# Channel slots of a fused attention and spectral-mix kernel: second pair's scores behind the first's

## The chip, the cores and the metric

The kernel runs on one core of a Trainium2 chip. The metric is the time on the device in microseconds (us); lower is better. Three runs of a kernel give its median, and one more execution was profiled.

## What is computed

Inputs q, k, v are (8, 12, 448, 64): batch 8, 12 heads, 448 positions, head width 64. Everything is float32.

```python
scores = cap * tanh(q @ k.T / sqrt(64) / cap)        # cap = 30
attn = exp(scores - max(scores)); attn /= sum(attn) + 1e-9
x = (attn @ v)                                       # heads side by side: (8, 448, 768)
theta = x @ w_theta
y = w_tok_r @ (x * cos(theta)) + w_tok_i @ (x * sin(theta))
u = x + y
out = u + max(u @ w_ch, 0)
```

## The kernel before, in words

The work is a list of slots. Slot s computes the scores of "step" s, which is four heads: two pairs i = 0, 1 of two heads h each. Beside them stands a share of the other work of one batch b. From slot 4 on three slots belong to each batch: part 0 computes theta, part 1 the token mix (mx), part 2 the channel product (ch). Three steps fill the 768 columns of a later batch. The words of a script (the lists PARTS and OTHER) give the order in which instructions are queued; each engine works through its own in that order. PARTS[2] is the script of slots 9, 12, 15, 18 and 21, which are called channel slots here; slots 6 and 24 have scripts of their own.

Words of the script that matter here:

- S0 to S3: score products of the four "bursts" of a slot. S0 holds chunks (0, 0) and (0, 1), that is pair 0 and its first and second 128 positions of k. S1 holds (0, 2) and None, the last 64 positions of both pairs. S2 holds (1, 0) and (1, 1), S3 holds (1, 2). A chunk is three products per head: k high x q high, k low x q high, k high x q low; None is one product in full float32.
- t0 to t3 and e0 to e3: ScalarE's tanh out of the banks and exp in place, of a burst each.
- V0, W, Vr: attn @ v of the step before (accumulators named a); cV0, cV1: ScalarE's copies of them to tiles X.
- a0a to a1b and F0, F1: VectorE adds up exp over the chunks, transposes and sums (folds). Rb: a small product of folds with diagonal gives the sums r; I inverts them and spreads them by DMA (bc); N and N- multiply X by bc.
- Pa1, Pb1: the high and low halves of q and of k of the slot's second pair; Pa0, Pb0: of the next slot's first pair. For an odd k both halves are VectorE's.
- u0 to u5: high half (ScalarE) and low half (VectorE) of the channel product's input; X0 to X5 the same for the next batch's theta.
- C0 to C5: channel product, 18 matmuls of 128x448 each; c0 to c5: its end on VectorE, and the DMA out.

Banks: psS is one tile of four banks (tag s) for S0, S1 and S2; psM has four single banks that a, r, mx, th, ch and S3's two tiles use in turn. The halves of k have one room each (tags kh, kl), so the second pair's k can be halved only when the first pair's last product has read them. Other halves, raw q and k, X, and bc come from 22 small rooms, handed out in the order in which they come free. The cap is 30, so the branch without the maximum runs (general is False).

Of the kernel before, what the change touches and what calls it, by code (L numbers as in the profile page):

```python
# [38 lines left out]
FLIP = (1,)  # L39

FOLD = (0, 1, 2)

FILL = {"branch": 10, "S0": 2, "t0": 8, "t1": 4}

# [34 lines left out]
def softcap_attn_then_spectral_mix(ctx, tc, qk2, v, cap, w_theta, w_tok, w_ch, outT):  # L79
# [16 lines left out]
    theta_words = w_theta.bitcast(I32).rearrange("m p j (n two) -> m p j n two", two=2)  # L96
    w_theta, w_ch = (w.rearrange("m p j n -> m p (j n)") for w in (w_theta, w_ch))

    singles = const.tile([P, 8], F32, name="singles")
    cap_sb, qscale, quarter, curve, wide_cap = (singles[:, n : n + 1] for n in range(5))  # L100
    wide_cap = wide_cap[:1, :].bitcast(I32)
    ones_sb = singles[:, 5:]
    nc.sync.dma_start(cap_sb, cap.broadcast_to([P, 1]))

    nc.vector.tensor_scalar(cap_sb.bitcast(I32), cap_sb.bitcast(I32), 0x7FFFFFFF, None, op0=ALU.bitwise_and)
# [24 lines left out]
    def load_consts():  # L130
        nc.gpsimd.memset(ones_sb[:, :1], 1.0)
        nc.gpsimd.memset(ones_sb[:, 1:], 0.0)
        for i in range(2):
            nc.gpsimd.memset(ones_sb[i * D : (i + 1) * D, i + 1 : i + 2], 1.0)
        nc.gpsimd.memset(diagonal, 0.0)
        for m in range(4):
            nc.gpsimd.affine_select(out=diagonal, in_=diagonal, pattern=[[0, 2], [-1, 32]], compare_op=ALU.not_equal, fill=1.0, base=-32 * m, channel_multiplier=1)
# [125 lines left out]


    BURSTS = (((0, 0), (0, 1)), ((0, 2), None), ((1, 0), (1, 1)), ((1, 2),))

    def load_raw(k, part, last=False):
        t = raw[k, part] = small.take([P, S], F32, f"{'qk'[part]}{k}", last=last)
# [16 lines left out]
    def prep_q(k):  # L285

        if 2 * WHOLE <= k < 2 * NS:
            Q[k, "q"] = halves(raw[k, 0], [P, S], small.take, f"q{k}", by_scalar(k))

    def prep_k(k):  # L290

        if 2 * WHOLE <= k < 2 * NS:
            t = raw.pop((k, 1))
            Q[k, "k"] = halves(t[:, :REST], [P, REST], lambda shape, dtype, name: wk.tile(shape, dtype, tag=f"k{name[-1]}", name=name, bufs=1), f"k{k}", by_scalar(k))
            if k % 2 == 0:
                Q[k, "r"] = wk.tile([P, S - REST], F32, tag="kr", name=f"r{k}", bufs=1)
                nc.vector.tensor_copy(Q[k, "r"], t[:, REST:])
            small.give(t)
            if k + 1 < 2 * NS:
                load_raw(k + 1, 1, k % 2 == 0 and by_scalar(k) and k > 2 * LEAD + 6)  # L300

    def scores(s, n):
        if n == 3 and s not in (1, LEAD + 1):
            t = spt[s, n] = [psM.tile([P, 512], F32, tag="m", name=f"s{s}_{n}{h}") for h in range(2)]
        else:
            t = spt[s, n] = psS.tile([P, 2, 2, 512], F32, tag="s", name=f"s{s}_{n}")
        for u, what in sorted(enumerate(BURSTS[n]), key=lambda at: at[1] is not None):
            for i in (0, 1) if what is None else what[:1]:
                k = 2 * s + i
                rows, cols = (slice(i * D, (i + 1) * D), slice(REST, S)) if what is None else (slice(0, P), slice(what[1] * P, (what[1] + 1) * P))  # L310
                out = [t[h][rows] if isinstance(t, list) else t[rows, u, h] for h in range(2)]
                if what is None and (k, "r") in Q:
                    products = ((Q.pop((k, "r")), raw[k, 0]),)
                elif what is None or s < WHOLE:
                    products = ((raw[k, 1][:, cols], raw[k, 0]),)
                else:
                    kk, qq = Q[k, "k"], Q[k, "q"]
                    products = [(kk[a][:, cols], qq[c]) for a, c in ((0, 0), (1, 0), (0, 1))]
                for m, (kk, qq) in enumerate(products):
                    for h in range(2):  # L320
                        rows = slice(h * D, (h + 1) * D)
                        nc.tensor.matmul(out[h][:, :S], kk[rows], qq[rows], start=m == 0, stop=m == len(products) - 1)  # L322
        k = 2 * s + n // 2
        if n in ((1, 3) if s else (1, 2)) and s < WHOLE:
            for part in range(2):
                small.give(raw.pop((k, part)))
        elif s >= WHOLE and n % 2:
            for t in Q.pop((k, "q")):
                small.give(t)
            if n == 1:  # L330
                for i in range(2):
                    small.give(raw.pop((k + i, 0)))
                if k + 2 < 2 * NS:
                    load_raw(k + 2, 0)
                    load_raw(k + 3, 0)

    def direct(s):
        return state["general"] or s < DIRECT

    def tanh(s, n):  # L340
        m = len(BURSTS[n])
        if m == 2:
            pp = large.take([P, 2, 2, S], F32, f"p{s}_{n}", EXPS if s < LEAD - 1 else None, s >= LEAD and n != 2)
            users[s, n] = [pp, {0: {"V0"}, 1: {"Vr", "V0"}, 2: {"W"}}[n] | (({"Ra", "Rb"}, {"Ra"}, {"Ra", "Rb"})[n] if direct(s) else set())]
        else:
            pp = wk.tile([P, 1, 2, S], F32, tag="p1", name=f"p{s}_{n}", bufs=1)
        for u, what in enumerate(BURSTS[n]):
            U[s, what] = pp[:, u]
        t = spt.pop((s, n))
        for h, each in enumerate(t if isinstance(t, list) else ()):  # L350
            nc.scalar.activation(pp[:, 0, h], each[:, :S], AF.Tanh, scale=qscale)
        if not isinstance(t, list):
            nc.scalar.activation(pp, t[:, :m, :, :S], AF.Tanh, scale=qscale)  # L353
        U[s, "t", n] = pp

    def used(s, word):
# [75 lines left out]
    def sums(s, word):  # L432
        if folded(s):
            if word == "Rb":
                r = state["r"] = psM.tile([P, 512], F32, tag="m", name=f"r{s}")
                for i in range(2):
                    nc.tensor.matmul(r[i * D : (i + 1) * D, : 2 * S // 32], diagonal.rearrange("p a j -> p (a j)"), folds[:, i], start=True, stop=True)
            return
        if not direct(s):
            if word == "Ra":  # L440
                return
            rounds, last = [([pst.pop((s, i)) for i in range(2)], False)], True
        else:
            rounds = [([U[s, (i, c)] for i in range(2)], False) for c in ((0, 2) if word == "Ra" else (1,))]
            if word == "Ra":
                rounds.append(([U[s, None]] * 2, True))
            last = word == "Rb"
        first = word == "Ra" or not direct(s)
        if first:
            state["r"] = psM.tile([P, 512], F32, tag="m", name=f"r{s}")  # L450
        r = state["r"]
        for n, (tiles, rest) in enumerate(rounds):
            for i in range(2):
                for h in range(2):
                    m = 32 * (2 * i + h)
                    nc.tensor.matmul(r[m : m + 32, :S], ones_sb[:, (i + 1 if rest else 0)][:, None].broadcast_to([P, 32]), tiles[i][:, h, :],  # L456
                                     start=first and n == 0, stop=last and n == len(rounds) - 1)

    def invert(s):
        r = state.pop("r")  # L460
        ri = small.take([P, S], F32, f"ri{s}") if direct(s) and not state["general"] else wk.tile([P, S], F32, tag="ps", name=f"ri{s}", bufs=2)
        if not folded(s):
            nc.vector.transpose(out=ri, in_=r[:, :S])
        few = wk.tile([P, S // 32], F32, tag="few", name=f"few{s}", bufs=1)
        each = ri.rearrange("p (c j) -> p c j", j=32)[:, :, 0]
        if state["general"]:
            nc.vector.tensor_scalar_add(few, each, 1e-9)
            nc.vector.reciprocal(few, few)
        elif folded(s):
            for m in range(4):  # L470
                rows, n = slice(32 * m, 32 * m + 32), S // 32
                nc.vector.reciprocal(few[rows], r[rows, n * (m % 2) : n * (m % 2) + n])  # L472
        else:
            nc.vector.reciprocal(few, each)
        nc.vector.transpose(out=ri, in_=few.unsqueeze(2).broadcast_to([P, S // 32, 32]))
# [12 lines left out]

    XHL = {}

    def split_x(b, j, name):
        if j % 2 == 0:
            XHL[name, b, j // 2] = large.take([P, 2, 2, S], F32R, f"{name}{b}_{j}")
        t = XHL[name, b, j // 2][:, j % 2]
        nc.scalar.copy(t[:, 0, :], X[b, j])
        nc.vector.tensor_tensor(t[:, 1, :], X[b, j], t[:, 0, :].bitcast(F32), op=ALU.subtract)  # L496

    def proj(b, wh, wl, m, name, of):
        acc = psM.tile([P, 512], F32, tag="m", name=f"{name}{b}_{m}")
# [117 lines left out]
    def chan_out(b, m):  # L617
# [15 lines left out]
    )  # L633
    OTHER = {
        0: "v S0 t0 q0 q1 w0 e0 S1 t1 S3 e1 w1 S2 t2 Vr^ e2 V0^ t3 S0> w2 e3 w3",
# [16 lines left out]
    def pipeline(general):  # L652
        state["general"] = general
        nc.scalar.activation(curve, quarter, AF.Tanh)
        def run(s, b, word):
# [63 lines left out]
                    fold(s, i)  # L719
            elif name == "w":  # L720
                weights(WEIGHTS.get((s, i), ""))
            elif name == "u":
                split_x(b, i, "us")
            elif name == "X":
                if b + 1 < B:
                    split_x(b + 1, i, "xs")
# [78 lines left out]
```

## Time and profile before

| | |
|---|---|
| median of 3 runs | 867.83 us (867.19 to 867.86) |
| profiled execution, own time | 867.0 us |
| its span, first to last instruction | 865.2 us |
| TensorE busy | 857.3 us, 99% of the span |
| VectorE busy | 716.5 us, 83% |
| ScalarE busy | 593.3 us, 69% |
| GpSimd busy | 112.5 us, 13% |
| granted TensorE clock | 0.999 of full speed |

Engines in the rows: PE is TensorE's matmuls, PEld its weight loads, DVE is VectorE, ACT ScalarE, POOL GpSimd, SP SyncE. A row of a timeline says start, length, engine, line of the code, operation, output <- inputs, shapes, how many instructions were merged, and in brackets how long the engine stood idle before it and what ended that. Ends of matmuls are modelled, so a matmul's start is the firmer number. The chain that ended last is followed back from the last instruction.

### The profile page before, as it was taken

How to read it: one execution, taken by the hardware profiler on the slowest of the kernel's cores; microseconds unless marked ns; L12 is line 12 of the kernel's file. 1: busy time of each engine (PE TensorE's matmuls, PEld its weight loads, DVE VectorE, ACT ScalarE, POOL GpSimd, SP SyncE). 2: the span in 40 equal slices, each digit the busy share in tenths (PEclk: the TensorE clock that was granted, in tenths of full speed). 3: DMA queues.
4: the chain of work that ended last, by engine and by line, in shares of the span. 5: the costliest groups of instructions: out<-in, count | busy, mean ns of one | idle time of the engine just before them, and what ended most of it. 6: DMA issues, size and time to landing. Idle time of an engine off the chain costs nothing.

```text
span 865.2 us, 13288 instructions
## 1 busy us (share of the span) xinstructions
PE 857.3 (99%) x4756; PEld 644.8 (75%) x4756; DVE 716.5 (83%) x1160; ACT 593.3 (69%) x693; POOL 112.5 (13%) x228
## 2 busy tenths in 40 slices
PE   9999999999999999999999999999999999999997
PEld 4335676867878778678787787787787877879996
DVE  5988989999888898888987899869979789886741
ACT  6898977679865797648957488655977379834420
POOL 1121342102200031001110013000130003100300
PEclk9999999999999999999999999999999999999999
DMA  8686286632522234223322324233142222311401
GB/s 314 198 303 216 81 236 206 231 108 59 155 75 75 86 103 118 88 78 102 111 87 86 118 64 121 64 94 118 54 139 86 86 86 72 110 44 31 141 12 56
DMA packets 51883, 99.74 MB, mean 115 GB/s; under 512 B 11232, under 2 KB 42592, under 8 KB 51808
## 3 DMA queue, kind: packets, MB, share of 16 engines
q1 hardware_dynamic: 38304, 58.13, 21.8%
q0 software_dynamic: 9184, 29.20, 11.1%
q10 hardware_dynamic: 4320, 11.47, 4.3%
q8 instruction: 39, 0.64, 0.3%
q14 instruction: 36, 0.29, 0.1%
HBM read 54.72 MB, written 11.01 MB: 76 GB/s over the span
## 4 chain that ended last, share of the span: by engine, by line
PE 98%; ACT 1%; DVE 0%; issue 0%; POOL 0%; POOLq 0%
PE s L322 15%; PE a L424 13%; PE mx L604 8%; PE mx L606 8%; PE mx L605 8%; PE th L503 7%; PE ch L503 7%; PE th L504 7%; PE th L505 7%; PE ch L505 7%; PE ch L504 7%; PE a L418 2%; PE r L456 2%; ACT p L353 1%; PE fill L128 1%; PE a L411 1%
## 5 line engine op out<-in xcount | busy, mean ns | idle before, releaser
L353 ACT ACTIVATE p<-s,singles 128x1792 f32<-128x1792 f32 (+1 forms) x54 | 93.3, 1728 | 87.7 <-PE s L322 87.4
L573 POOL DMA_DIRECT2D t<-g_row x148 | 74.5, 510 | 542.7 <-ACT z L527 215.6
L604 PE MATMUL mx<-wtk_h,zh 128*128 128x448 f32 x336 | 125.1, 372 | 0.7 <-ACT zh L587 0.7
L606 PE MATMUL mx<-wtk_h,zl 128*128 128x448 f32 x336 | 124.0, 369 | 0.0
L605 PE MATMUL mx<-wtk_l,zh 128*128 128x448 f32 x336 | 123.4, 367 | 0.0
L366 ACT ACTIVATE p<-p,singles 128x1792 f32<-128x1792 f32 (+1 forms) x76 | 118.2, 1556 | 1.4 <-PE a L424 0.6
L503 PE MATMUL ch<-us,wch_h 128*128 128x448 f32 x288 | 106.9, 371 | 0.0
L503 PE MATMUL th<-xs,wth_h 128*128 128x448 f32 x288 | 106.7, 371 | 0.0
L504 PE MATMUL th<-xs,wth_h 128*128 128x448 f32 x288 | 105.5, 366 | 0.0
L505 PE MATMUL th<-xs,wth_l 128*128 128x448 f32 x288 | 105.5, 366 | 0.0
L504 PE MATMUL ch<-us,wch_h 128*128 128x448 f32 x288 | 105.3, 366 | 0.0
L505 PE MATMUL ch<-us,wch_l 128*128 128x448 f32 x288 | 105.3, 366 | 0.0
L424 PE MATMUL a<-p,v 128*64 128x448 f32 x492 | 101.8, 545 | 0.0
L594 DVE TENSOR_TENSOR zl<-t,zh 128x512 fp32r<-128x512 f32 x88 | 52.9, 618 | 27.3 <-ACT zh L587 26.0
L424 PEld LDWEIGHTS a<-p,v 128*64 128x64 f32 x492 | 32.9, 136 | 56.5 <-issue 51.1
L604 PEld LDWEIGHTS mx<-wtk_h,zh 128*128 128x128 f32 x336 | 63.1, 188 | 12.5 <-issue 3.7
L587 ACT CAST zh<-t 128x512 fp32r<-128x512 f32 x88 | 46.7, 559 | 36.7 <-DMA t<-g_row 13.2
L606 PEld LDWEIGHTS mx<-wtk_h,zl 128*128 128x128 f32 x336 | 63.1, 188 | 7.6 <-DVE zl L594 1.7
L605 PEld LDWEIGHTS mx<-wtk_l,zh 128*128 128x128 f32 x336 | 63.1, 188 | 5.5
L503 PEld LDWEIGHTS th<-xs,wth_h 128*128 128x128 f32 x288 | 54.0, 188 | 9.5 <-issue 3.5
L503 PEld LDWEIGHTS ch<-us,wch_h 128*128 128x128 f32 x288 | 54.0, 187 | 8.4 <-DVE few L472 1.5
L504 PEld LDWEIGHTS th<-xs,wth_h 128*128 128x128 f32 x288 | 54.0, 188 | 4.9 <-DVE xs L496 0.2
(598 smaller groups left out, 1652.4 us busy)
## 6 DMA issues: line engine op xcount, KB each, us to landing
v<-in_v ACTq DMA_DIRECT2D x22, 448.0 KB, 3.3
k<-in_qk SPq DMA_DIRECT2D x41, 224.0 KB, 3.5
bc<-ri SPq DMA_DIRECT2D x82, 112.0 KB, 2.4
q<-in_qk SPq DMA_DIRECT2D x37, 224.0 KB, 3.3
t<-g_row SPq DMA_DIRECT2D x148, 56.0 KB, 2.4
t<-g_row POOLq DMA_DIRECT2D x148, 56.0 KB, 2.3
out_dram<-x SPq DMA_DIRECT2D x36, 224.0 KB, 1.9
x_row<-in_qk SPq DMA_DIRECT2D x18, 224.0 KB, 2.8
```

Of the source, the lines that this page charges most:

```text
L322: nc.tensor.matmul(out[h][:, :S], kk[rows], qq[rows], start=m == 0, stop=m == len(products) - 1)
L353: nc.scalar.activation(pp, t[:, :m, :, :S], AF.Tanh, scale=qscale)
L366: nc.scalar.activation(pp, pp, AF.Exp, scale=cap_sb)
L424: nc.tensor.matmul(acc_of["a", s, i][h * D : (h + 1) * D, :S], vt[s][:, 6 * i + 3 * h + c, :], U[s, (i, c)][:, h, :], start=first and c == ...
L503: nc.tensor.matmul(acc[:, :S], wh[:, j, ms], t[:, 0, :], start=j == 0, stop=False)
L504: nc.tensor.matmul(acc[:, :S], wh[:, j, ms], t[:, 1, :], start=False, stop=False)
L505: nc.tensor.matmul(acc[:, :S], wl[:, j, ms], t[:, 0, :], start=False, stop=j == NJ - 1)
L573: queue.dma_start(t[32 * m : 32 * m + 32, d * S : (d + 1) * S], f[32 * d : 32 * d + 32, m * S : (m + 1) * S])
L594: nc.vector.tensor_tensor(zl, tokens(b, j)[:, c0:c1], zh.bitcast(F32), op=ALU.subtract)
L604: nc.tensor.matmul(acc[:, :S], zh, wtk_h[:, c, :], start=c == 0, stop=False)
L605: nc.tensor.matmul(acc[:, :S], zh, wtk_l[:, c, :], start=False, stop=False)
L606: nc.tensor.matmul(acc[:, :S], zl, wtk_h[:, c, :], start=False, stop=c == NC2 - 1)
```

## The change

The scripts of the other slots stay as they are. In PARTS[2] the word u is cut into uh (the high half) and ul (the low half), and S2 and S3 stand right behind S1, ahead of all six C. In the channel slots (once(s) is true for 9, 12, 15, 18, 21) further:

- psS's four banks become one lasting tile, four. S2 has only chunk (1, 0) and goes to two psM banks; S3 has (1, 2) and then (1, 1), in four. t1 is two ACTIVATEs (None first), t2 two of 448 columns, t3 two of 896.
- Rb's r of the step before goes to a bank of four, and is read at once: own_half makes the 14 wanted columns of each partition by two VectorE operations with a mask (evens), into a part of folds. In other slots with folds own_half runs at I. The one reciprocal over 128 partitions takes the place of four over 32.
- The second pair's k halves get two small rooms, taken with the q halves at Pa1.

```diff
+ONCE = (2,)
-    singles = const.tile([P, 8], F32, name="singles")
+    singles = const.tile([P, 10], F32, name="singles")
+    evens = singles[:, 8:]
+        for m in range(4):
+            nc.gpsimd.memset(evens[32 * m : 32 * m + 32, m % 2 : m % 2 + 1], 1.0)
...
+    four = psS.tile([P, 2, 2, 512], F32, tag="s", name="four")
+
+    def once(s):
+        return s > LEAD + 2 and s < NS and (s - LEAD) % NP2 in ONCE
...
     def prep_q(k):
             Q[k, "q"] = halves(raw[k, 0], [P, S], small.take, f"q{k}", by_scalar(k))
+            if once(k // 2) and k % 2 and (k // 2 - LEAD) % NP2:
+                Q[k, "rooms"] = [small.take([P, S], F32R, f"k{k}{part}") for part in "hl"]
     def prep_k(k):
-            Q[k, "k"] = halves(t[:, :REST], [P, REST], lambda shape, dtype, name: wk.tile(shape, dtype, tag=f"k{name[-1]}", name=name, bufs=1), f"k{k}", by_scalar(k))
+            if once(k // 2) and k % 2:
...
+                rooms = iter(Q[k, "rooms"])
+                Q[k, "k"] = halves(t[:, :REST], [P, REST], lambda shape, dtype, name: next(rooms)[:, :REST], f"k{k}", by_scalar(k))
+            else:
...
     def scores(s, n):
-        if n == 3 and s not in (1, LEAD + 1):
+        if once(s) and n == 2:
             t = spt[s, n] = [psM.tile([P, 512], F32, tag="m", name=f"s{s}_{n}{h}") for h in range(2)]
+            chunk(s, (1, 0), t)
+        elif once(s) and n == 3:
+            for u, what in ((1, (1, 2)), (0, (1, 1))):
+                chunk(s, what, [four[:, u, h] for h in range(2)])
+        elif n == 3 and s not in (1, LEAD + 1):
+            t = spt[s, n] = [psM.tile([P, 512], F32, tag="m", name=f"s{s}_{n}{h}") for h in range(2)]
+            chunk(s, (1, 2), t)
         else:
-            t = spt[s, n] = psS.tile([P, 2, 2, 512], F32, tag="s", name=f"s{s}_{n}")
+            for u, what in sorted(enumerate(BURSTS[n]), key=lambda at: at[1] is not None):
+                chunk(s, what, [four[:, u, h] for h in range(2)])
...
     def tanh(s, n):
+        if once(s) and n == 1:
+            for u in (1, 0):
+                nc.scalar.activation(pp[:, u], four[:, u, :, :S], AF.Tanh, scale=qscale)
+        elif once(s) and n == 3:
+            nc.scalar.activation(pp[:, 0], four[:, 1, :, :S], AF.Tanh, scale=qscale)
+            nc.scalar.activation(U[s, (1, 1)], four[:, 0, :, :S], AF.Tanh, scale=qscale)
...
     def sums(s, word):
-                r = state["r"] = psM.tile([P, 512], F32, tag="m", name=f"r{s}")
+                r = state["r"] = four[:, 0, 0] if once(s + 1) else psM.tile([P, 512], F32, tag="m", name=f"r{s}")
...
+                if once(s + 1):
+                    own_half(r)
+    few = folds[:, 0, : S // 32]
+
+    def own_half(r):
+        n = S // 32
+        nc.vector.tensor_scalar_mul(few, r[:, :n], evens[:, :1])
+        nc.vector.scalar_tensor_tensor(few, r[:, n : 2 * n], evens[:, 1:], few, op0=ALU.mult, op1=ALU.add)
     def invert(s):
-        few = wk.tile([P, S // 32], F32, tag="few", name=f"few{s}", bufs=1)
         elif folded(s):
-            for m in range(4):
-                rows, n = slice(32 * m, 32 * m + 32), S // 32
-                nc.vector.reciprocal(few[rows], r[rows, n * (m % 2) : n * (m % 2) + n])
+            if not once(s + 1):
+                own_half(r)
+            nc.vector.reciprocal(few, few)
...
     PARTS[2]
-        "S0 t0 u0 u1 V0 u2 u3 e0 u4 u5 W Ra Rb Vr cV0 cV1 v w0 Pa1 S1 Pb1 q0 t1 N- C0 c0 e1 a0a w1 C1 c1 I S2 S3 t2 t3 a0b F0 C2 c2 w2 N e2 C3 Pa0 c3 Pb0 q1 X0 X1 a1a"
-        " C4 c4 e3 X2 X3 w3 a1b F1 X4 C5 X5 c5",
+        "S0 t0 uh0 uh1 V0 uh2 uh3 e0 ul0 W Ra Rb Vr uh4 Pa1 S1 Pb1 t1 S2 cV0 uh5 cV1 v w0 ul1 ul2 ul3 ul4 ul5 S3 q0 I a0a e1 a0b t2 t3 N- C0 c0 w1 N F0 C1 e2 c1 a1a e3 a1b C2 c2 w2 F1 Pa0 Pb0 q1 X0 X1 C3 c3 X2 X3"
+        " C4 c4 w3 X4 C5 X5 c5",
```

chunk(s, what, out) holds the loop that stood in scores, with the same products; split_x gets the argument parts, "h", "l" or both. The score tiles of a chunk are freed as before, and the two k rooms are given back with the q halves at S3.

## Rows read from the trace of the kernel before

**Rows 1.** The page: busy time of each engine, and the chain that ended last.
```profile
PE 857.3 (99%) x4756; PEld 644.8 (75%) x4756; DVE 716.5 (83%) x1160; ACT 593.3 (69%) x693; POOL 112.5 (13%) x228
...
PE 98%; ACT 1%; DVE 0%; issue 0%; POOL 0%; POOLq 0%
```

**Rows 2.** List of waits, TensorE alone, whole span (line, releaser: total, times, longest).
```profile
PE fill L128 <- POOL singles L132: 0.9, 1, 0.9
...
PE s L322 <- ACT p L353: 0.2, 1, 0.2
```

**Rows 3.** Windows: slots s=12 and s=18, length, then each engine's busy time.
```profile
346.81:380.05 33.24, 33.24 (x191) 25.79 (x190) 27.89 (x47) 19.00 (x23) 0.00 (x0) 1.00 0.27 82
...
553.93:586.93 33.00, 33.00 (x189) 25.74 (x188) 26.25 (x45) 19.01 (x23) 0.00 (x0) 1.00 0.26 77
```

**Rows 4.** Timeline of TensorE in slot s=12 around the score products.
```profile
355.06 0.36 PE L322 MATMUL s<-q24h,k24l 64*128 64x448 f32 x2
355.26 0.37 PE L322 MATMUL s<-q24l,k24h 64*128 64x448 f32 x2
355.56 0.47 PE L503 MATMUL ch<-us,wch_h 128*128 128x448 f32 x1
...
362.82 0.37 PE L505 MATMUL ch<-us,wch_l 128*128 128x448 f32 x1
363.12 0.47 PE L322 MATMUL s<-q25h,k25h 64*128 64x448 f32 x2
363.43 0.36 PE L322 MATMUL s<-q25h,k25l 64*128 64x448 f32 x2
...
364.85 0.36 PE L322 MATMUL s<-q25l,k25h 64*128 64x448 f32 x2
365.14 0.47 PE L503 MATMUL ch<-us,wch_h 128*128 128x448 f32 x1
```

**Rows 5.** Timeline of TensorE: the sums' product and small scores (s=12, s=21).
```profile
352.79 0.37 PE L437 MATMUL r<-folds,diagonal 128*64 128x28 f32 x4
...
354.28 0.54 PE L322 MATMUL s<-x_row,k 64*64 64x448 f32 x1
...
663.77 0.55 PE L437 MATMUL r<-folds,diagonal 128*64 128x28 f32 x4
```

**Rows 6.** Timeline of VectorE in slot s=12.
```profile
351.72 1.08 DVE L398 TENSOR_REDUCE folds<-ft 128x28 f32<-128x896 f32 x1
352.72 2.22 DVE L496 TENSOR_TENSOR us<-x,us 128x448 fp32r<-128x448 f32 x4
...
355.93 0.38 DVE L278 CAST q25h<-x_row 128x448 fp32r<-128x448 f32 x1
...
357.27 0.56 DVE L279 TENSOR_TENSOR k25l<-k,k25h 128x384 fp32r<-128x384 f32 x1
...
363.77 1.03 DVE L472 RECIPROCAL few<-r 32x14 f32<-32x14 f32 x4
```

**Rows 7.** Timeline of ScalarE in slot s=12.
```profile
354.46 0.96 ACT L429 COPY x<-a 128x448 f32<-128x448 f32 x2
355.67 1.76 ACT L353 ACTIVATE g_row<-s,singles 128x1792 f32<-128x1792 f32 x1 [0.25 <-PE s L322]
...
366.31 1.15 ACT L351 ACTIVATE p<-s,singles 128x448 f32<-128x448 f32 x2
```

**Rows 8.** Timeline of all engines at the program's start.
```profile
0.94 5.01 PE L128 MATMUL fill<-singles 128*32 128x112 f32 x24 [0.94 <-POOL singles L132]
0.97 0.24 POOL L134 MEMSET singles<- 64x1 f32 x2
...
4.09 0.12 DVE L109 TENSOR_SCALAR singles<-singles 1x1 int32<-1x1 f32 x1
...
8.01 1.75 ACT L353 ACTIVATE p<-s,singles 128x1792 f32<-128x1792 f32 x1 [1.59 <-PE s L322]
...
9.81 2.03 PE L322 MATMUL s<-x_row 64*64 64x448 f32 x12 [0.18 <-ACT p L353]
```

More of the change, by code (lines that the diff above doesn't have):

```diff
@@ L293, in prep_k @@
             t = raw.pop((k, 1))
-            Q[k, "k"] = halves(t[:, :REST], [P, REST], lambda shape, dtype, name: wk.tile(shape, dtype, tag=f"k{name[-1]}", name=name, bufs=1), f"k{k}", by_scalar(k))
+            if once(k // 2) and k % 2:
+                if (k, "rooms") not in Q:
+                    Q[k, "rooms"] = [small.take([P, S], F32R, f"k{k}{part}") for part in "hl"]
+                rooms = iter(Q[k, "rooms"])
+                Q[k, "k"] = halves(t[:, :REST], [P, REST], lambda shape, dtype, name: next(rooms)[:, :REST], f"k{k}", by_scalar(k))
+            else:
+                Q[k, "k"] = halves(t[:, :REST], [P, REST], lambda shape, dtype, name: wk.tile(shape, dtype, tag=f"k{name[-1]}", name=name, bufs=1), f"k{k}", by_scalar(k))
             if k % 2 == 0:
@@ L302, in scores @@
     def scores(s, n):
-        if n == 3 and s not in (1, LEAD + 1):
+        if once(s) and n == 2:
             t = spt[s, n] = [psM.tile([P, 512], F32, tag="m", name=f"s{s}_{n}{h}") for h in range(2)]
-        else:
-            t = spt[s, n] = psS.tile([P, 2, 2, 512], F32, tag="s", name=f"s{s}_{n}")
[L307 to L322, printed above, removed]
+            chunk(s, (1, 0), t)
[5 more added lines that the diff above has]
+            chunk(s, (1, 2), t)
+        else:
+            for u, what in sorted(enumerate(BURSTS[n]), key=lambda at: at[1] is not None):
+                chunk(s, what, [four[:, u, h] for h in range(2)])
         k = 2 * s + n // 2
@@ L327, in scores @@
         elif s >= WHOLE and n % 2:
-            for t in Q.pop((k, "q")):
+            for t in Q.pop((k, "q")) + (Q.pop((k, "rooms")) if (k, "rooms") in Q else []):
                 small.give(t)
@@ L335, in scores, with chunk @@
                     load_raw(k + 3, 0)
+    def chunk(s, what, out):
+        for i in (0, 1) if what is None else what[:1]:
+            k = 2 * s + i
+            rows, cols = (slice(i * D, (i + 1) * D), slice(REST, S)) if what is None else (slice(0, P), slice(what[1] * P, (what[1] + 1) * P))
+            if what is None and (k, "r") in Q:
+                products = ((Q.pop((k, "r")), raw[k, 0]),)
+            elif what is None or s < WHOLE:
+                products = ((raw[k, 1][:, cols], raw[k, 0]),)
+            else:
+                kk, qq = Q[k, "k"], Q[k, "q"]
+                products = [(kk[a][:, cols], qq[c]) for a, c in ((0, 0), (1, 0), (0, 1))]
+            for m, (kk, qq) in enumerate(products):
+                for h in range(2):
+                    half = slice(h * D, (h + 1) * D)
+                    nc.tensor.matmul(out[h][rows, :S], kk[half], qq[half], start=m == 0, stop=m == len(products) - 1)
     def direct(s):
@@ L348, in tanh @@
             U[s, what] = pp[:, u]
[L349 to L353, printed above, removed]
+        if once(s) and n == 1:
[4 more added lines that the diff above has]
+            nc.scalar.activation(U[s, (1, 1)], four[:, 0, :, :S], AF.Tanh, scale=qscale)
+        elif (s, n) in spt:
+            for h, each in enumerate(spt.pop((s, n))):
+                nc.scalar.activation(pp[:, 0, h], each[:, :S], AF.Tanh, scale=qscale)
+        else:
+            nc.scalar.activation(pp, four[:, :m, :, :S], AF.Tanh, scale=qscale)
         U[s, "t", n] = pp
@@ L489, in softcap_attn_then_spectral_mix, with split_x @@
     XHL = {}
-    def split_x(b, j, name):
-        if j % 2 == 0:
+    def split_x(b, j, name, parts="hl"):
+        if j % 2 == 0 and "h" in parts:
             XHL[name, b, j // 2] = large.take([P, 2, 2, S], F32R, f"{name}{b}_{j}")
         t = XHL[name, b, j // 2][:, j % 2]
-        nc.scalar.copy(t[:, 0, :], X[b, j])
-        nc.vector.tensor_tensor(t[:, 1, :], X[b, j], t[:, 0, :].bitcast(F32), op=ALU.subtract)
+        if "h" in parts:
+            nc.scalar.copy(t[:, 0, :], X[b, j])
+        if "l" in parts:
+            nc.vector.tensor_tensor(t[:, 1, :], X[b, j], t[:, 0, :].bitcast(F32), op=ALU.subtract)
     def proj(b, wh, wl, m, name, of):
@@ L721, in run @@
                 weights(WEIGHTS.get((s, i), ""))
-            elif name == "u":
-                split_x(b, i, "us")
+            elif name in ("u", "uh", "ul"):
+                split_x(b, i, "us", name[1:] or "hl")
             elif name == "X":
```

## The prediction, made before the result was known

> **What bounds the kernel now.** I read the page first: TensorE is busy for 99% of the span, and the chain that ended last is 98% TensorE [rows 1]. So only what lengthens or shortens TensorE's own stream counts; VectorE (83%) and ScalarE (69%) matter where they make TensorE wait. The list of TensorE's waits has three entries of 1.8 us in all, of which the first and last are shown [rows 2]. A stream of that kind can still lose time between instructions, so I next took the time of single channel slots from the windows: the five slots that the change touches (s = 9, 12, 15, 18, 21) take 33.0 to 33.3 us each, of which two are shown [rows 3]. Then I read the starts of matmuls in slot s=12. Inside a stage successive products start 0.20 us apart (355.06, 355.26). Where the shape of the array changes, from the scores' 64*128 to the channel's 128*128 or back, the step before the change is 0.29 or 0.30 (355.26 to 355.56, 362.82 to 363.12, 364.85 to 365.14) and the step behind it 0.31 (363.12 to 363.43) [rows 4]. A change of shape thus costs 0.30 + 0.31 - 2 x 0.20 = 0.2 us, without showing as a wait.
>
> **What the new order removes.** Before, the stretch behind the first pair's scores goes scores, C0 C1, scores, C2 to C5: three changes of shape. The new script puts S2 and S3 right behind S1, with C0 to C5 in one run: one change. No matmul is added or dropped (24 score and 108 channel products, as before). Two changes less are 2 x 0.20 = 0.40 us a slot, and 5 x 0.40 = 2.0 us in the kernel. That is the whole of the gain that I find.
>
> **What the new order can make late.** The second pair's scores now start 7.65 us earlier: at 355.26 + 0.20 = 355.47 (from unrounded steps) in place of 363.12 [rows 4]. Three things must be ready.
>
> The sums' product r goes to a scores' bank, and two new VectorE operations (own_half) must read it before S1's (0, 2) chunk writes there. They are queued behind one low half of the channel input (ul0). The fold's sum ends at 352.80 and ul0 starts at 352.72, so it ends at about 353.34, and VectorE can take the next at about 353.26, at the step of four in 2.22 us [rows 6]. The four r products start at 352.79 and are over at 353.16 [rows 5]. No row shows own_half. Nearest are the four reciprocals out of PSUM, four in 1.03 us, so 0.26 each [rows 6]; I take 2 x 0.26 = 0.52, end at 353.78. Bounds: 0.12 each, the least VectorE operation [rows 8], and 0.38 each, the cast of 448 columns [rows 6]; a gain is excluded at this place, since nothing stood there before. S1's (0, 2) chunk starts near 354.75, a step of 0.31 before 355.06 [rows 4], so r's new bank costs nothing: the cover is the rest products and the small scores, and without it the two operations would cost up to 0.5 us. What is queued behind own_half is the halving of the second pair.
>
> Second, q25's and k25's halves, which were done at 355.93 to 357.83, 1.90 us of VectorE [rows 6]. The small rooms free them from waiting until S1 has read the first pair's k halves. Started at 353.78 they end at 355.68. The low half of k is wanted by the second pair of products, at 355.67, and the hand-over takes about 0.05, as where a score follows a tanh (8.01 + 1.75 = 9.76, then 9.81) [rows 8]: late by 0.06, at the bounds 0 and 0.30.
>
> Third, the banks. S2 goes to two free ones of the four, which m4 and m5 gave up: they stand ahead of the fold on VectorE, which ended at 352.80 [rows 6]. S3 goes back to the scores' tile, so it waits for S1's tanh, which is cut in two: first the half of the small scores, then that of (0, 2). The small scores end at 354.28 + 0.54 = 354.82 [rows 5]; a tanh starts 0.04 behind its matmul (355.26 + 0.37 = 355.63 [rows 4], then 355.67 [rows 7]), so 354.86. ScalarE is free by then: with both casts it was through at 354.46 [rows 7], and the two copies out of the a banks now stand behind the tanh. A tanh of 896 columns lies between 0.63 (448, two in 1.15 overlapping by 0.11) and 1.76 (1792) [rows 7]: 1.00. The first half ends at 355.86, the second, from 355.75, at 356.75. S3's (1, 2) chunk wants its bank at 355.47 + 0.61 = 356.08: in time by 0.2. The (1, 1) chunk wants its bank at 356.69 and gets it at 356.80: 0.11 late. The 0.06 of the k half lies within this 0.11, since the tanh's end stands fixed.
>
> A rule of the Trainium skill speaks against the cut: ScalarE: Activation LUTs, section "What ACT_TABLE_LOAD costs", gives each ACTIVATE with one pointer operand a fixed 280 ns beside 0.833 ns a column, and an overlap of 93 ns. By it the two halves, as an estimate, take 1.96 us and not 1.89, the wait is 0.18, and the kernel gains 1.1 us in place of the sum below. The trace's 0.63 at 448 columns is a little under the 0.65 of that rule, and I stay with the trace.
>
> **Parts at nothing.** C0 wants a bank: the first copy out of a starts behind the second tanh half, at 356.64, and takes about 0.5 (two in 0.96 [rows 7]), so 357.2; C0 starts at about 357.5. If that 0.3 were gone, C0 would wait by as much. Its low halves ul1 to ul5 come from 355.6 on at 0.53 each and are wanted at 0.61 each from 358 on. In slots of all three kinds, four reciprocals (1.03) become two operations and one reciprocal (about 0.8); that is VectorE time beside TensorE's stream. With the two k rooms 21 of the 22 small rooms are taken until S3 (at the slot's start 10 X tiles, 3 raw, 2 q halves and 2 bc; then 2 q and 2 k halves); the next pair's q loads on SP's queue then go into rooms that S1 has just read, so they start at 355.6 and not before, and the next k load and the sums' four carries behind them: nothing of theirs is wanted for 5 us or more. The earlier fold F1 gives VectorE slack at the end of the slot, where TensorE waits for nothing. Four small memsets at the program's start run beside the fills; the fills begin at 0.94 before the last memset of their tile at 0.97 [rows 8].
>
> **The sum.** 0.40 - 0.11 = 0.29 a slot, 5 x 0.29 = 1.45 us. The profiled execution took 867.0 around a span of 865.2; it would be 865.6. The median shown, 867.83, lies 0.8 above the profiled one; from it the forecast is 866.4. A difference under 0.2% (1.7 us) can hardly be told from none in this kernel.
>
> **Rivals.** *Full gain (17%).* The tanh halves or k halves come in time, and TensorE's lateness at r, four products over 0.55 us in s=21 and 0.37 in s=12 [rows 5], shrinks because the reciprocals' step is shorter: 867.8 - 2.0 - 0.4 at most = 865.4 to 865.9. Against it: the tanh halves are a chain of ScalarE work that cannot start before the small scores end.
>
> *Eaten (23%).* With own_half at 0.38 each the wait is 0.30, the gain 0.1 a slot; with other lateness on VectorE, which runs without a break from before the slot to 357.8, nothing is left: 867.0 to 868.3. For it: the margins above are all under 0.3 us.
>
> *One order over the whole scores' tile (8%), the slower one.* The four banks are now one lasting tile. If its readers and writers are kept apart as a whole, and not by bank, the first tanh half starts at S1's end, 355.67, the second ends at 357.56, and S3 waits from 356.08 to 357.6: 1.5 us a slot against 0.40, 5 x 1.1 = 5.6 us slower, 873.4. It decides from 0.4 us of delay on. Against it: the fills begin while the same tile's other columns are still to be written [rows 8]; but that tile is no bank of PSUM, and no row shows one used in part.
>
> *The forecast (45%)*, by itself 865.8 to 867.0; the last 7% go to small losses between eaten and slower, up to 870, of which more than half pass 0.2%.
>
> **Range and chances.** The range 865.2 to 868.6 holds the first three cases (85%); s=12 and s=18 do the same work in 33.24 and 33.00 us [rows 3], a spread that lies within it. Faster by over 0.2% (under 866.1): the full gain and a quarter of the forecast's case, 0.29. Slower by over 0.2%: 0.08 + 0.04 = 0.12. Within: 0.59.
>
> **What would show it.** In a slot of the changed kernel: 24 score products in one run; one change of shape ahead of C0; C0 to C5 without a break; the slot about 0.3 us shorter; a step over 0.2 us ahead of the last six score products; the k halves ending near 355.68 on this clock. A wait of TensorE on the tanh of over 0.4 us, or a first tanh half that starts only at the end of all of S1, would make the prediction wrong, and so would slots of part 0 and 1 that change length.

## The result, and the profile after

The changed kernel takes 873.65 us (median of 4 runs, 873.39 to 874.28) against 867.67 for the kernel before (4 runs). The ratio is 1.0071, 95% interval 1.0053 to 1.0088: 6.0 us slower. The forecast was 866.4 with a range up to 868.6; the rival "one order over the whole scores' tile", which held 8%, had said 873.4. The profiled execution took 873.39, its span is 871.6 against 865.2.

The page's line of busy time and its chain, which answer [rows 1]:

```profile
PE 857.7 (98%) x4756; PEld 645.3 (74%) x4756; DVE 710.8 (82%) x1143; ACT 593.2 (68%) x703; POOL 111.8 (13%) x232
...
PE 96%; ACT 2%; issue 1%; DMA 0%; POOL 0%; DVE 0%; ACTq 0%; POOLq 0%
```

TensorE is as busy as before, 857.7 us, in a span 6.4 us longer, and ScalarE now holds 2% of the chain. The list of TensorE's waits, in answer to [rows 2]:

```profile
PE four L360 <- ACT g_row L376: 6.7, 5, 1.3
PE fill L131 <- POOL singles L135: 0.9, 1, 0.9
```

One new wait, five times, 6.7 us in all: products into the scores' tile wait for ScalarE's line 376, which is t1 in two halves. The program's start (fill) is as it was. The windows of slots s=12 and s=18, in answer to [rows 3] (length, then busy time of PE, PEld, DVE, ACT and POOL, then the granted clock as a share of full speed, and last the busy share of the DMA engines and the GB/s that they moved):

```profile
348.59:383.01 34.42, 33.10 (x190) 25.70 (x189) 32.54 (x51) 19.03 (x25) 0.00 (x0) 1.00 0.26 81
557.99:592.38 34.39, 33.05 (x189) 25.67 (x188) 32.20 (x51) 19.04 (x25) 0.00 (x0) 1.00 0.26 81
```

The five channel slots take 34.39, 34.42, 34.49, 34.39 and 34.66 us where they took 33.07, 33.24, 33.11, 33.00 and 33.28: 6.6 us more in all, so the slots of the other parts account for nothing. Inside s=12, TensorE's timeline, in answer to [rows 4, 5]:

```profile
354.57 0.28 PE L468 MATMUL four<-folds,diagonal 128*64 128x28 f32 x4
...
355.99 0.54 PE L360 MATMUL four<-q,k 64*64 64x448 f32 x1
356.45 0.47 PE L360 MATMUL four<-q24h,k24h 64*128 64x448 f32 x2
356.76 0.36 PE L360 MATMUL four<-q24h,k24l 64*128 64x448 f32 x2
356.96 0.37 PE L360 MATMUL four<-q24l,k24h 64*128 64x448 f32 x2
357.17 0.37 PE L360 MATMUL s<-q25h,k25h 64*128 64x448 f32 x2
357.37 0.43 PE L360 MATMUL s<-q25h,k25l 64*128 64x448 f32 x2
357.64 0.37 PE L360 MATMUL s<-q25l,k25h 64*128 64x448 f32 x2
359.33 0.47 PE L360 MATMUL four<-q25h,k25h 64*128 64x448 f32 x2 [1.32 <-ACT g_row L376]
359.64 0.37 PE L360 MATMUL four<-q25h,k25l 64*128 64x448 f32 x2
...
360.45 0.37 PE L360 MATMUL four<-q25l,k25h 64*128 64x448 f32 x2
360.75 0.47 PE L544 MATMUL ch<-us,wch_h 128*128 128x448 f32 x1
```

ScalarE over the same time, in answer to [rows 7]:

```profile
357.37 1.01 ACT L376 ACTIVATE g_row<-four,singles 128x896 f32<-128x896 f32 x1 [1.50 <-PE four L360]
...
358.28 1.00 ACT L376 ACTIVATE g_row<-four,singles 128x896 f32<-128x896 f32 x1
```

And VectorE, in answer to [rows 6]:

```profile
353.42 1.08 DVE L429 TENSOR_REDUCE folds<-ft 128x28 f32<-128x896 f32 x1
354.42 0.62 DVE L537 TENSOR_TENSOR us<-x,us 128x448 fp32r<-128x448 f32 x1
354.95 0.23 DVE L496 TENSOR_SCALAR folds<-four,singles 128x14 f32<-128x14 f32 x1
355.22 0.23 DVE L497 SCALAR_TENSOR_TENSOR folds<-four,singles,folds 128x14 f32<-128x14 f32 x1
355.37 0.38 DVE L287 CAST q25h<-q 128x448 fp32r<-128x448 f32 x1
...
356.71 0.56 DVE L288 TENSOR_TENSOR k25l<-k,k25h 128x384 fp32r<-128x384 f32 x1
```

Read the three together. The first half of t1 takes the banks of the small scores, whose last product ends at 355.99 + 0.54 = 356.53. ScalarE stands idle, yet the tanh starts at 357.37: 0.04 behind the end of the last product of all of S1 (356.96 + 0.37 = 357.33). The second half ends at 359.28, and the first product of S3, whose own two banks the first half had left at 358.38, starts at 359.33, 0.05 behind the second. Both sides start as if they waited for the whole tile.

The slot adds up in that stretch. From S2's start to C0, 18 products take 360.75 - 357.17 = 3.58 us, where before they took 365.14 - 363.12 = 2.02 [rows 4]: 1.56 more. Of it 1.49 is the wait (the step into S3 is 359.33 - 357.64 = 1.69 instead of 0.20), 0.06 the step at 357.37 (0.27: the low half of k, see below), and 0.10 a step of 0.31 instead of 0.20 right behind the wait (359.33 to 359.64); 0.09 goes off, since S2 now stands behind scores of its own shape. C0 to C5 take 383.01 - 360.75 = 22.26, where they took 7.56 and 14.91 [rows 3, 4]: 0.21 less. S1's (0, 2) takes 0.72 in place of 0.81, and r's products 0.22 in place of 0.30, a step that differs from slot to slot. 1.56 - 0.21 - 0.09 - 0.08 = 1.18, and the slot is 34.42 - 33.24 = 1.18 longer.

### The profile page after: what moved, and what is told of

It reads as the page before. It is cut to its first block, busy times and chain, and to the rows that moved or that the text cites. A ratio compares the mean times of both kernels' runs of the same rounds, so it can differ in the third digit from the quotient of the medians.

```text
span 871.6 us, 13297 instructions
## 1 busy us (share of the span) xinstructions
PE 857.7 (98%) x4756; PEld 645.3 (74%) x4756; DVE 710.8 (82%) x1143; ACT 593.2 (68%) x703; POOL 111.8 (13%) x232
## 4 chain that ended last, share of the span: by engine, by line
PE 96%; ACT 2%; issue 1%; DMA 0%; POOL 0%; DVE 0%; ACTq 0%; POOLq 0%
PE a L455 13%; PE four L360 13%; PE mx L645 8%; PE mx L647 8%; PE mx L646 8%; PE th L544 7%; PE ch L544 7%; PE th L545 7%; PE ch L546 7%; PE th L546 7%; PE ch L545 7%; PE a L449 2%; PE r L489 2%; PE s L360 1%; ACT g_row L376 1%; ACT p L384 1%
## 5 line engine op out<-in xcount | busy, mean ns | idle before, releaser
L384 ACT ACTIVATE p<-four,singles 128x1792 f32<-128x1792 f32 (+1 forms) x49 | 84.6, 1726 | 96.1 <-PE four L360 95.8
L544 PEld LDWEIGHTS th<-xs,wth_h 128*128 128x128 f32 x288 | 54.1, 188 | 9.7 <-issue 4.7
L546 PEld LDWEIGHTS ch<-us,wch_l 128*128 128x128 f32 x288 | 53.9, 187 | 5.1
```

The lines of the kernel that those rows point to most:

```text
L384: nc.scalar.activation(pp, four[:, :m, :, :S], AF.Tanh, scale=qscale)
L544: nc.tensor.matmul(acc[:, :S], wh[:, j, ms], t[:, 0, :], start=j == 0, stop=False)
L546: nc.tensor.matmul(acc[:, :S], wl[:, j, ms], t[:, 0, :], start=False, stop=j == NJ - 1)
```

## The experiments

Theory: the scores' tile is kept in order as a whole, so S3 waits for the second tanh half, which can start only 0.91 behind the end of S1. Rivals: cutting the tanh costs the time by itself; the time lies in the moved work (own_half, C0's bank, the rooms); or the order is by bank and ScalarE was held up by something else.

**Two tiles in place of one.** The four banks become two tiles of two banks, so that each half has an order of its own. All tanh of two chunks are cut in two, in the other slots as well.

```diff
-    four = psS.tile([P, 2, 2, 512], F32, tag="s", name="four")
+    four = [psS.tile([P, 2, 512], F32, tag=f"s{u}", name=f"four{u}") for u in range(2)]
...
-            nc.scalar.activation(pp, four[:, :m, :, :S], AF.Tanh, scale=qscale)
+            for u in (1, 0) if n == 1 else range(m):
+                nc.scalar.activation(pp[:, u], four[u][:, :, :S], AF.Tanh, scale=qscale)
```

> The changed kernel, but the lasting scores' tile is two tiles of two banks each, and every tanh of two chunks is two ACTIVATEs, one out of each tile. Theory (the one tile is ordered as a whole): the first tanh half of t1 starts when the small scores end, some 0.85 us earlier than in the changed kernel, each chunk of S3 waits for its own half alone, TensorE's wait ahead of S3 falls from 1.5 us to under 0.2 us a slot, and the time is 866.0 to 867.2 us. Rival (the wait comes from the tanh's own length or its place in ScalarE's queue, not from the order kept over the tile): the wait stays over 1 us and the time over 872 us.

Measured: 867.00 us (11 runs) against 867.42, ratio 0.9992 (0.9983 to 1.0001). The loss is gone. ScalarE in its slot s=12:

```profile
356.99 1.01 ACT L382 ACTIVATE g_row<-four,singles 128x896 f32<-128x896 f32 x1 [1.43 <-PE four L360]
...
357.90 1.00 ACT L382 ACTIVATE g_row<-four,singles 128x896 f32<-128x896 f32 x1
```

And TensorE:

```profile
356.39 0.54 PE L360 MATMUL four<-q,k 64*64 64x448 f32 x1
...
357.36 0.37 PE L360 MATMUL four<-q24l,k24h 64*128 64x448 f32 x2
...
358.64 0.38 PE L360 MATMUL four<-q25l,k25h 64*128 64x448 f32 x2
358.96 0.47 PE L360 MATMUL four<-q25h,k25h 64*128 64x448 f32 x2
359.26 0.37 PE L360 MATMUL four<-q25h,k25l 64*128 64x448 f32 x2
```

The first tanh half starts at 356.99, 0.06 behind the small scores (356.39 + 0.54) and ahead of the end of S1 (357.73). S3's (1, 2) chunk no longer waits; (1, 1) comes 0.12 late (a step of 0.32, and a second one of 0.30 behind it). C0's bank is free in time: the copy that gives it up ends at 358.79 + 0.53 = 359.32, C0 starts at 359.76. In the profiled executions the five slots sum to 0.35 us less than before, 0.07 each: most of the gain that was sought is eaten again, and the times cannot tell the rest from none.

**The cut alone, in the kernel before.**

```diff
-            nc.scalar.activation(pp, t[:, :m, :, :S], AF.Tanh, scale=qscale)
+            for u in (1, 0) if n == 1 else range(m):
+                nc.scalar.activation(pp[:, u], t[:, u, :, :S], AF.Tanh, scale=qscale)
```

> The kernel before with one edit: every tanh of two chunks is two ACTIVATEs out of the same one tile. It prices the cut alone, some 70 ACTIVATEs more of about 0.15 us on ScalarE. Theory: ScalarE has room, 867.2 to 868.2 us. Rival (cutting costs, as late tanhs reach TensorE): over 868.7 us.

Measured: 868.84 us (10 runs), ratio 1.0017 (1.0008 to 1.0027). The theory's 867.2 to 868.2 is missed and the rival's mark of 868.7 just reached: cutting every tanh costs 1.4 us while a tile is ordered as a whole. Its list of TensorE's waits has

```profile
PE s L322 <- ACT p L354: 1.1, 5, 0.3
```

that is, scores that wait for a cut tanh, five times where the kernel before has one such wait of 0.2 [rows 2]. The first and the last of the five:

```profile
10.03 2.03 PE L322 MATMUL s<-x_row 64*64 64x448 f32 x12 [0.33 <-ACT p L354]
...
54.67 2.03 PE L322 MATMUL s<-q,k 64*64 64x448 f32 x12 [0.19 <-ACT p L354]
```

All five lie in the first 55 us of the program, where the changed kernel cuts no tanh. In the channel slots no product waits for a cut tanh, and the five of them sum to only 0.2 us more than before. So the cut by itself does not make the 6 us.

**The changed kernel with t1 in one piece in the channel slots.**

```diff
-        if once(s) and n == 1:
-            for u in (1, 0):
-                nc.scalar.activation(pp[:, u], four[:, u, :, :S], AF.Tanh, scale=qscale)
-        elif once(s) and n == 3:
+        if once(s) and n == 3:
```

> The changed kernel with t1 of the channel slots as one ACTIVATE of 1792 columns again. Theory (ordered as a whole, so the cut buys nothing): S3 waits for the end of all of t1 in both, one ACTIVATE of 1.76 us ends 0.13 us sooner than two in 1.89, so 5 x 0.13: 872.8 to 873.3 us. Rival (S3's first chunk waits for its own half in the changed kernel): without the cut that chunk waits longer and the time is 873.7 us or more.

Measured: 873.27 us (5 runs), ratio 1.0065 (1.0051 to 1.0079), within what the theory gave. The rival's mark (873.7) is only 0.4 away, less than the interval, so the time does not decide between them; the trace does. The wait stays, a little shorter:

```profile
PE four L360 <- ACT g_row L381: 5.9, 5, 1.2
```

and in s=12:

```profile
357.54 0.37 PE L360 MATMUL s<-q25l,k25h 64*128 64x448 f32 x2
359.08 0.47 PE L360 MATMUL four<-q25h,k25h 64*128 64x448 f32 x2 [1.17 <-ACT g_row L381]
```

With an order by bank, one tanh of all four banks must have been worse than two halves. It is not: the step into S3 falls from 1.69 to 359.08 - 357.54 = 1.54, since one tanh of 1792 columns is over sooner than two of 896.

**C0 in the waiting time.** S3 is put behind C0, so that the wait is filled with 18 channel products.

```diff
-... ul1 ul2 ul3 ul4 ul5 S3 q0 I a0a e1 a0b t2 t3 N- C0 c0 w1 N F0 C1 ...
+... ul1 ul2 ul3 ul4 ul5 q0 a0a e1 a0b t2 N- I C0 S3 t3 c0 w1 N F0 C1 ...
```

> The changed kernel with C0 ahead of S3 in the script (and I and N- ahead of C0), so that 18 channel products cover the wait for t1. Two changes of shape a slot come back. Theory: the wait of 1.5 us and the 0.1 us of the restart are gone and 0.40 us of shape changes are back, 5 x 1.2 us: 867.3 to 868.2 us, about the kernel before. Rival (S3 waits for something that C0 does not cover, a bank or the k halves): over 870 us.

Measured: 878.55 us (4 runs), ratio 1.0131 (1.0116 to 1.0147): the theory's time was wrong. The time is the rival's and the reason is a bank, but it is C0 that waits for it, and not S3, whose wait for t1 is gone from the list as the theory had it.

```profile
PE ch L544 <- ACT x_row L460: 5.3, 3, 1.8
PE ch L544 <- ACT x L460: 3.5, 2, 1.8
```

S2 and the two accumulators a fill the four single banks, and the copy that frees one of them stands behind t1 on ScalarE (line 460 is cV0 and cV1). So C0 starts 2.58 us behind the start of S2, 0.4 later than S3 did (2.16), and the two changes of shape are back. In the changed kernel C0's bank is free from 359.17 + 0.53 = 359.70 on, by ScalarE's copy, and C0 starts at 360.75; without S3's wait alone, C0 would have come to about 359.2 and waited there (an estimate from these rows). With two tiles the whole of t1 and the copy come earlier, and the bank is in time by 0.4.

**Two tiles, with what is late moved.** On top of the two tiles: the small scores ahead of the last attn @ v products, q25's halves ahead of own_half, ul0 behind the halves of k.

```diff
-... e0 ul0 W Ra Rb Vr uh4 Pa1 S1 Pb1 t1 S2 ...
+... e0 W Ra Pa1 Rb Sn Vr uh4 S1 Pb1 ul0 t1 S2 ...
...
+                if what is not None or not once(s):
...
+            elif name == "Sn":
+                chunk(s, None, [four[1][:, h] for h in range(2)])
```

> The changed kernel with two tiles for the scores, and in the channel slots the small scores ahead of the last attn @ v products (both 64*64), the halving of the second pair's q ahead of own_half, and the first low half of the channel input behind the halving of k. Theory (each tile is ordered as a whole; what is left of the wait is ScalarE's second tanh half, 0.1 us late, and the low k half, 0.06 late, each with a restart of about 0.1): the first tanh half starts about 0.8 us earlier, the second at the end of (0, 2), both lates are gone, each of the five slots gets 0.2 to 0.26 us shorter than with two tiles alone, 24 score products stand in one run with no step over 0.22 behind the first, and the time is 865.6 to 866.2, ratio about 0.998. Rival (the steps behind a wait are not caused by it, or the lost time lies elsewhere): as with two tiles alone, 866.8 to 867.3.

Measured: 867.07 us (11 runs) against 867.28, ratio 0.9998 (0.9989 to 1.0007): the time that the rival gave. One half of the expectation held: k comes in time, no step of S2 is over 0.21. The other did not. ScalarE's list of waits has

```profile
ACT g_row L383 <- PE a L448: 6.0, 5, 1.3
```

and TensorE's timeline in s=12

```profile
356.94 0.37 PE L361 MATMUL four<-q25l,k25h 64*128 64x448 f32 x2
357.33 0.47 PE L361 MATMUL four<-q25h,k25h 64*128 64x448 f32 x2
357.64 0.37 PE L361 MATMUL four<-q25h,k25l 64*128 64x448 f32 x2
```

The tanh writes into the room g_row, which still holds the exp that the last attn @ v products read (a<-g_row, line 448). Those now stand behind the small scores, so the tanh starts as late as before, and (1, 1) is 0.19 late instead of 0.12. What was won at k is lost there.

**All but the order, in the old place.** S2 and S3 stand behind C1 again; the lasting tile, r in a scores' bank, own_half at Rb and the cut t1 and t3 stay; the k halves have their old rooms.

```diff
-        "S0 t0 uh0 uh1 V0 uh2 uh3 e0 ul0 W Ra Rb Vr uh4 Pa1 S1 Pb1 t1 S2 cV0 ...
+        "S0 t0 u0 u1 V0 u2 u3 e0 u4 u5 W Ra Rb Vr cV0 cV1 v w0 Pa1 S1 Pb1 q0 t1 N- C0 c0 e1 a0a w1 C1 c1 I S2 S3 t2 t3 ...
```

> All of the change but its order and the small rooms of the k halves: in the channel slots S2 and S3 stand where they stood before (S2 and S3 behind C1), with one lasting scores' tile, r in a scores' bank, own_half, one reciprocal, t1 and t3 in two halves. Theory (the loss is S3's wait for all of t1 and that alone, which needs S3 right behind S1): the time of the kernel before, 867.4 to 868.2, with up to 0.5 us from the small scores' wait for own_half. Rival (own_half, the cut tanh, the earlier read of r or the lasting tile cost time by themselves): over 869.

Measured: 884.40 us (4 runs), ratio 1.0187 (1.0166 to 1.0207), the largest miss of the study.

```profile
PE four L360 <- DVE folds L497: 12.0, 5, 2.4
```

VectorE in s=12:

```profile
357.12 2.22 DVE L537 TENSOR_TENSOR us<-x,us 128x448 fp32r<-128x448 f32 x4
359.25 0.62 DVE L537 TENSOR_TENSOR us<-x_row,us 128x448 fp32r<-128x448 f32 x1
359.79 0.62 DVE L537 TENSOR_TENSOR us<-x,us 128x448 fp32r<-128x448 f32 x1
360.32 0.23 DVE L496 TENSOR_SCALAR folds<-four,singles 128x14 f32<-128x14 f32 x1
360.58 0.23 DVE L497 SCALAR_TENSOR_TENSOR folds<-four,singles,folds 128x14 f32<-128x14 f32 x1
```

TensorE's products behind own_half:

```profile
357.48 0.98 PE L449 MATMUL a<-g_row,v 64*64 64x448 f32 x8
360.87 0.59 PE L360 MATMUL four<-q,r 64*64 64x448 f32 x2 [2.41 <-DVE folds L497]
```

own_half is queued behind six low halves and is over at 360.81. The small scores start at 360.87 in place of about 358.28 (s=12 of the changed kernel: 0.80 behind the first of the eight), though they go to other banks than r: the whole-tile order a second time, now between VectorE and TensorE, for 2.6 us a slot. That is 13 us in five slots; nearly all of the rest of the profiled execution's 19 (886.43) is TensorE's clock (last section).

**The same, with r in a single bank and own_half at I.**

```diff
-                r = state["r"] = four[:, 0, 0] if once(s + 1) else psM.tile([P, 512], F32, tag="m", name=f"r{s}")
+                r = state["r"] = psM.tile([P, 512], F32, tag="m", name=f"r{s}")
...
-                if once(s + 1):
-                    own_half(r)
...
-            if not once(s + 1):
-                own_half(r)
+            own_half(r)
```

> As the kernel with the old place of S2 and S3, but the sums' product r goes to one of the four single banks again and own_half stands at I. What is left of the change: the lasting scores' tile, S2 in two single banks and S3 in the scores' tile, t1 and t3 in two halves, own_half with one reciprocal. Theory (in the old place the loss was the wait of the small scores for own_half, which stood behind six low halves on VectorE; the other parts cost nothing): the time of the kernel before, 867.2 to 868.2, and no wait of TensorE on a scores' tile over 0.3 us in the channel slots. Rival (one of the other parts costs time in the old place): over 869.

Measured: 867.90 us (10 runs) against 866.97, ratio 1.0008 (0.9998 to 1.0017), as the theory has it. All that its list shows on a scores' tile is

```profile
PE four L360 <- ACT p L384: 0.2, 1, 0.2
```

So the lasting tile, the exchanged banks, the cut tanh in five slots, own_half and the one reciprocal cost, in the old order, nothing that can be told from none (at most 1.5 us by the interval).

## Why the prediction was wrong

The step that failed is the one on the banks: "The small scores end at 354.28 + 0.54 = 354.82 [...] so 354.86", and with it "S3's (1,2) chunk wants its bank at 355.47 + 0.61 = 356.08: in time by 0.2". It takes for granted that banks of one tile are handed over one by one. The tile is handed over whole: the first tanh half started at the end of all of S1, as the prediction's last paragraph named for the case that it is wrong, and S3 waited 1.49 us for the second half, in each of the five slots. In the sum, the 0.11 of the wait measured 1.49, with 0.06 and 0.10 beside it. With two tiles and the same script nothing is lost (867.00). That the order belongs to the tile, and not to the size of the tanh, is shown by the uncut t1, where the wait stays (873.27); that it holds between other engines too, by the small scores behind own_half.

The Trainium skill, PSUM — Partial Sum Buffer, section "PSUM bank collisions raise a hardware error", asks for guards by bank (with quadrants of partitions) and not by address. Here the program waits more widely than that, by tile, and two tiles of two banks took the wait away: the chip did not need it.

Where the chances went astray: that case held 8%, and its price of 5.6 us came near the 6.0 measured, its wait (1.5 a slot, measured 1.49) nearer still. What spoke against it, the fills that begin while another column of their tile is still to be written [rows 8], came from a tile outside PSUM with readers and writers of other columns, and the text itself said that no row shows a PSUM tile used in part. A cost that no row bears out and on which 7 us hang wanted a larger share and a range that reached it.

The other steps, one by one:

- *Two changes of shape fewer, 0.40 a slot*: the mechanism is right, the size 0.3. (0, 2) became 0.09 shorter and S2 with S3 0.09, as 0.1 each; C0 to C5 became 0.21 shorter in s=12, but 0.13 on the mean of the five slots, since before, in four of them, C0 with C1 (7.51 in place of 7.56 us) or C2 to C5 (14.83 in place of 14.91) had run at slightly shorter steps. The Trainium skill, TensorEngine Tiling (Array Packing), section "Tiling Modes", says that a change of mode drains the engine; the steps of 0.30 and 0.31 at a change, against 0.20 [rows 4], agree with it.
- *own_half, 0.52*: 0.42 (354.95 to the cast at 355.37), within its bounds, and before (0, 2) by 1.0. What the step left out is that the small scores, 0.86 earlier, wait for it as well.
- *The k half, 0.06 late*: 0.06, a step of 0.27, but by luck. The halves took 1.90 us, as computed, and own_half was 0.10 shorter, so k25l was over at 357.27, where the prediction's 355.68 is 357.38 on this clock (S2 starts at 357.17 in place of 355.47). With the hand-over of 0.05 that is 357.32, and its product stands at 357.37: in time, by the prediction's own reckoning. What waited was the load of the product's weights, which the step left out. The load after and before:

```profile
357.32 0.18 PEld L360 LDWEIGHTS s<-q25h,k25l 64*128 64x128 f32 x2 [0.18 <-DVE k25l L288]
...
363.22 0.19 PEld L322 LDWEIGHTS s<-q25h,k25l 64*128 64x128 f32 x2
```

  Before, it started 0.21 ahead of its product (363.43); here only 0.05. So k was wanted earlier than the prediction took it, and two errors made up for each other.
- *Two tanh halves, 1.89*: 1.91 (357.37 to 359.28). By the rule of the Trainium skill, ScalarE: Activation LUTs, section "What ACT_TABLE_LOAD costs", the estimate was 1.96; the trace's own rows were nearer.
- *(1, 1), 0.11 late*: with two tiles, where (1, 1) waits for its own half alone, 0.12.
- What no step had: TensorE pays 0.1 more on the first step behind a wait, as in the step of 0.31 behind S3's and that of 0.30 behind (1, 1)'s. With two tiles that makes 0.06 + 0.12 + 0.10 = 0.28 of loss against a gain of 0.3; the slots show 0.07 left: by bank, the outcome would have lain where the forecast's own range (to 867.0) and the rival "eaten" (from 867.0) meet.
- *Parts at nothing*: true together in the old place (867.90), with two conditions. The small rooms of k were not tried by themselves. Cutting the low halves off (ul1 to ul5) was no detail: without it own_half comes 2.6 us late.

Open: how the cut tanh in all slots of the kernel before makes 1.4 us, of which the list shows 0.9 as new waits, all at the program's start; and whether any order gets the full 0.3 a slot. No kernel here is faster than the one before by more than its interval.

## What to carry to other kernels

Before work is moved up to a buffer that "is half free", look at what the wait is attached to: here it was the tile, and splitting it in two turned a loss of 6.0 us (873.65 against 867.67) into no loss (867.00 against 867.42). Count what an instruction waits for on all sides, the output room of the tanh as much as its input banks, and ask of a wait that is removed which one lies right under it: behind S3's wait lay C0's bank, and behind the small scores the room g_row. A gain of 0.4 us a slot that rests on margins of 0.1 to 0.3 is eaten by the first one that fails, since each wait costs its own length and a restart.

## What the runs showed of the hardware

- TensorE's clock fell behind some of the longer waits. In the kernel with all but the order in the old place, TensorE had been almost idle (0.13 of 2 us busy, clock 1.00), then ran the small scores and (0, 2), and the first channel products followed at steps of 0.37 in place of 0.20. The windows of that stretch (columns as above):

```profile
359.00:361.00 2.00, 0.13 (x4) 0.13 (x6) 1.97 (x6) 0.65 (x2) 0.00 (x0) 1.00 0.62 188
361.30:363.40 2.10, 2.10 (x15) 0.98 (x8) 0.87 (x3) 0.42 (x1) 0.00 (x0) 0.76 0.04 10
363.40:365.40 2.00, 2.00 (x7) 1.77 (x6) 1.60 (x3) 1.97 (x3) 0.00 (x0) 0.50 0.71 229
```

  The granted clock goes 1.00, 0.76, 0.50; the last is the lower level, 1.2 GHz. Four of its five slots have such slow steps in the scores or in C0 and are 4.1 to 4.5 us longer than before; the fifth, without them, is 2.6 longer. The difference, summed over the four, is some 7 us. The fifth has the same wait of 2.4 in front, so the wait's length alone does not say whether the clock falls. The four executions took 882.20 and 882.58 us, with a mean granted clock of 0.998, and 886.21 and 886.43, with 0.993 and 0.990. In the kernel with C0 ahead of S3 the clock fell to 0.50 in one slot of five, behind a wait of 1.77, for nine products at 0.37: 1.5 us; behind the other four waits, of 1.75 and 1.76, it did not. In the changed kernel, with waits of 1.3, it did not (1.00 in both windows of its slots).
- The step behind a wait of TensorE is 0.1 longer than the others, in three kernels (0.31, 0.30 and 0.31 in the rows above). The list of waits doesn't count it.
- A product can be late by its weights, though they are written before it starts: see the load of k25l above (0.05 ahead of its product in place of 0.21, and 0.06 lost). With k in time, in the kernel with the small scores first, no step of these products is over 0.21.
